# Another order for the first quarter of a hand-ordered linear-attention and MLP kernel

## The chip, the cores and the metric

The kernel runs on one core of a Trainium2 chip. A core has TensorE (PE), which multiplies matrices into PSUM, VectorE (DVE), ScalarE (ACT), GpSimd (POOL), which can't read PSUM here and works in SBUF, and SyncE (SP), which in this kernel only issues DMAs. Each engine takes its own instructions in the order in which they were emitted and waits at semaphores for the others. The time is device microseconds of one execution, as the median of several; smaller is better.

## The reference

```python
# attention with a complex decay, per batch b (4) and head h (8); S = 768 steps, D = 48
mag = sqrt(a_re**2 + a_im**2);  scale = min(mag, 0.999) / (mag + 1e-6)
a_re_n, a_im_n = a_re * scale, a_im * scale
for t in range(S):
    S_re, S_im = ar * S_re - ai * S_im + k_t (x) v_t,  ar * S_im + ai * S_re
    y[t] = q_t @ S_re
# then, on x = y laid out as (4, 768, 384), d_model = 384
xn = (x - mean) / sqrt(var + 1e-6) * g_ln
out = x + relu(xn @ w_ch1) @ w_ch2          # 384 -> 1536 -> 384
```

## The kernel before, in words

The step-by-step recurrence is done in chunks of 128 steps. Two chunks make a pair; there are twelve pairs, three for each batch. For a pair the kernel needs the running sum of log|a| and the running phase over the chunk. In the names of the order table, P is the pair, n the chunk:

- `are.P`, `aim.P`, `q.P.c`, `k.P.c`, `vf.P.c`: loads on SP's queue (L452 and L404). Pair 0 has `are`, `aim` and all that follows up to `ks` and `qs` in two halves of four heads, 0.0 and 0.1.
- On ScalarE `ln` (log of a_re, L459) and `iv` (its inverse, L461); `r` = a_im / a_re (L295); `r2` its square; `u` = log(1 + r2) on ScalarE (L473); `l` and `lc` on VectorE (L477, L480): log|a|, clamped.
- `dec` (L488): matmuls with a triangle of ones sum it up; `e` and `en` (L492) are exp of plus and minus the sum, on ScalarE.
- `th` = arctan(r) (L496); `ph` (L503, L507): matmuls sum the phase, in turns, on top of what the pair before carried over; `car` (L517, L520) carries it on; `sin` (L525), `qt` (L532, a quarter turn by a matmul) and `cos` (L536).
- `ke`, `qe` = k * en, q * e and `ks`, `qs` = these times cos and sin (all through the helper line L295). `kT`, `qT` transpose them on TensorE (L613), `ksT`, `qsT` copy the result from PSUM (L292 on VectorE, L290 on ScalarE).
- `am` (L636) are the scores of a chunk, `atm` (L295) the masked scores, `gm` (L660) and `G` the state, `gs` its sum ahead of the decay, `y` (L697, L700) the chunk's output. `row` (L592, a small DMA), `dps` (L597) and `decc` bring the pair's decay into place.
- `bn` (L707, L708) mean and variance, `x` (L714, L717), `xtr`, `xT` its transpose (L734), `mm1` (L767), `relu` (L779, L781), `mm2` (L791), `rstd`, `oa`, `xr`, `ot` and the store `st`.
- `wl.0` and `wl.1` (L369, L371): GpSimd issues the loads of the two weights, w1b and w2b, with a cast. `wc` (L385) multiplies w1b by the layer norm's gain on VectorE, in nine pieces; `mm1` needs them.
- `warm.*` (L822, L826): matmuls whose result nobody reads, in places of TensorE's order where it would wait. `tab.log` and `tab.trig` (L831): loads of ScalarE's function table; logarithms and exponentials are in one, arc tangents and sines in the other.

The order of everything is a table, the string PLAN. A token is `name:engine`, with the PSUM bank behind the engine's letter (P, A, V, G, S) and, behind an @, an operation for which this one must wait besides its own data. The program emits the operations in the table's order, each on the named engine, so the table is the order of every engine's queue. Names of some kinds that aren't in the table aren't emitted: where `qe.1.0.1` is missing, `qe.1.0.0` does both chunks.

Buffers are rings (`are` and `aim` three deep, `vf` two, `e` and `en` two, `ks` and `qs` three). TensorE's eight PSUM banks are given out by the table.

Of the kernel before, what the change touches and what calls it, by code (L numbers as in the profile page):

```python
# [49 lines left out]
r2.0.0:V warm.12:P6 th.0.1:A warm.w18:P5 r2.0.1:V uthc:V warm.w11:P4 pad.ks.0:G@r2.0.0 th.1.0:A warm.w9:P4 q.0.1:S  # L50
warm.8:P1 warm.7:P6 r2.1.0:G warm.w36:P2 warm.3:P4 warm.4:P6 ph.0.1:P0 aim.2.0:S warm.w6:P5 ph.0.0:P6 k.0.0:S v.0:G
tab.log.2:A u.0.1:A warm.w8:P2 warm.w13:P5 k.0.1:S u.0.0:A warm.2:P2 car0.1:G@uth l.0.1:V warm.w30:P3 warm.w38:P2
u.1.0:A mask:G@r2.0.0 l.0.0:V q.1.1:S zrow.0:G@uth pad.ks.1:G@r2.0.0 lc.0.1:V ln.2.0:A l.1.0:V dec.0.1:P1 warm.11:P2
warm.w17:P5 e.0.1:A1 k.1.1:S warm.w12:P3 lc.0.0:V iv.2.0:A lc.1.0:V dec.0.0:P7 qe.0.1.0:G@lc.0.0 car.0.0:V6 dec.1.0:P4
q.1.0:S car.0.1:V0 en.0.1:A1 r.2.0:V qrow:G warm.w16:P2 en.0.0:A7 ph.1.0:P2 e.1.0:A4 q.2.1:S ke.0.0.0:V e.0.0:A7
warm.28:P1 are.3.0:S r2.2.0:V en.1.0:A4 warm.19:P7 warm.w4:P1 ke.0.1.0:V vf.1.0:S u.2.0:A warm.w0:P5 qe.0.0.0:V
warm.w40:P4 warm.w22:P7 car.1.0:V2 warm.w3:P7 k.1.0:S warm.5:P7 warm.w20:P5 l.2.0:V warm.w31:P7 warm.w23:P5 aim.3.0:S
warm.w21:P7 warm.w28:P1 qe.1.0.0:V tab.trig.3:A sin.0.1:A0 sin.0.0:A6 lc.2.0:V qt.0.1:P0 ks.0.1.1:V sin.1.0:A2 row.0:S
qs.0.1.1:V warm.w2:P7 warm.w19:P4 ks.0.0.1:V row.1:S qt.0.0:P6 qe.1.0.1:V cos.0.1:A0 qt.1.0:P2 vf.1.1:S cos.0.0:A6
ks.0.1.0:V dec.2.0:P0 qs.0.1.0:V cos.1.0:A2 ks.0.0.0:V k.2.1:S warm.14:P6@en.1.0 qs.0.0.0:V qs.0.0.1:V warm.0:P6  # L60
kT.0:P4 th.2.0:A qs.1.0.0:V qT.0:P6 warm.w34:P7 wl.0:G@qs.0.0.1 kT.1:P3 ksT.0:V4 qT.2:P2 k.2.0:S qsT.0:V6 qT.1:P5
ke.1.0.0:G q.2.0:S tab.log.4:A en.2.0:A0 qsT.2:V2 am.0:P6 are.4.0:S ksT.1:V3 qsT.1:A5 atm.0:V6 warm.27:P3 ks.1.0.0:G
warm.w14:P3 e.2.0:A0 am.1:P2 atm.1:V2 ln.3.0:A y.0:P6 gm.0:P0 dps.1:P7 warm.15:P1 warm.w33:P1 G.0:A0 warm.16:P5
warm.25:P1 qT.3:P1 decc.1:A7 bn.0:V6 iv.3.0:A gm.1:P0 y.1:P5 qsT.3:V1 aim.4.0:S x.0:A6 dps.0:P4 r.3.0:G kT.2:P7
bn.1:V5 decc.0:A4 xtr.0:P4 kT.3:P6 ksT.2:V7 ph.2.0:P2 G.1:V0 qe.2.0.1:G@ksT.2 tab.trig.5:A th.3.0:A ksT.3:V6 am.2:P0
ngl:G@ksT.2 sin.2.0:A2 warm.w37:P7 v.1:G atm.2:V0 warm.13:P7 am.3:P6 xT.0:A4 qt.2.0:P2 r2.3.0:G@ksT.3 x.1:A5 gm.2:P4
atm.3:V6 ph.3.0:P0 cos.2.0:A2 xr.0:G G.2:V4 warm.23:P2 are.5.0:S xtr.1:P2 car.3.0:A0 warm.9:P3 warm.w41:P6 sin.3.0:A0
gm.3:P4 wc.0.1:V y.2:P7 wc.1.0:V y.3:P5 xT.1:A2 wc.1.1:V wc.1.2:V vf.2.0:S qt.3.0:P0 wl.1:G@wc.1.1 bn.2:V7
mm1.0.1.0:P2 cos.3.0:A0 wc.0.0:V mm1.0.1.1:P2 vf.2.1:S wc.0.2:V x.2:A7 wc.2.2:V mm1.0.0.1:P0 wc.2.0:V relu.0.1:A2
wc.2.1:V bn.3:V5 mm1.0.0.0:P0 qe.2.0.0:G@wc.2.1 xtr.2:P3 aim.5.0:S x.3:V5 mm1.0.2.0:P6 ke.2.0.0:G@bn.3 xT.2:V3  # L70
xtr.3:P5 mm1.0.2.1:P6 xT.3:V5 tab.log.6:A u.3.0:A gs.3:V4 mm1.1.0.1:P2 qs.2.0.0:V relu.0.2:A6 mm1.1.1.0:P4 ks.2.0.0:V
relu.0.0:A0 mm1.1.1.1:P4 ks.2.0.1:V mm1.1.0.0:P2 l.3.0:V ln.4.0:A mm1.1.2.1:P0 relu.1.1:A4 relu.1.0:V2 kT.5:P6
mm1.1.2.0:P0 iv.4.0:A ksT.5:V6 qT.5:P4 relu.1.2:A0 lc.3.0:V qT.4:P3 r.4.0:G@ksT.5 qsT.5:V4 kT.4:P5 qsT.4:A3 dec.3.0:P6
ksT.4:V5 are.6.0:S am.5:P0 e.3.0:A6 rstd.0:G am.4:P2 atm.5:V0 r2.4.0:A mm2.0.0:P4 mm2.0.1:P4 atm.4:V2 u.4.0:A q.3.0:S
rstd.1:G@atm.5 mm2.2.0:P1 ln.5.0:A row.3:S mm2.0.2:P4 l.4.0:V q.3.1:S v.2:A mm2.2.1:P1 G.3:G ot.0:V4 mm2.2.2:P1
iv.5.0:A lc.4.0:V k.3.1:S gm.4:P5 en.3.0:A6 dec.4.0:P2 r.5.0:G G.4:V5 y.4:P4 oa.2:A1 st.0:S y.5:P0 bn.4:V4 mm2.3.0:P7
ln.6.0:A k.3.0:S ot.2:G bn.5:V0 mm2.1.0:P6 en.4.0:A2 x.4:V4 mm2.3.1:P7 e.4.0:A2 st.2:S r2.5.0:V vf.3.1:S mm2.1.1:P6
qe.3.0.0:V x.5:A0 row.4:S xtr.4:P2 qe.3.0.1:V iv.6.0:A mm2.3.2:P7 vf.3.0:S xr.3:G@qe.3.0.0 xT.4:V2 xtr.5:P5 u.5.0:A
mm2.1.2:P6 xr.1:G@qe.3.0.1 q.4.0:S xT.5:V5 ke.3.0.1:G ot.3:V7 mm1.2.0.0:P4 ot.1:V6 mm1.2.0.1:P4 aim.6.0:S rstd.2:G
qs.3.0.0:V k.4.0:S mm1.2.2.0:P2 tab.trig.7:A th.4.0:A ke.3.0.0:V mm1.2.2.1:P2 k.4.1:S relu.2.0:A4 ks.3.0.0:V ph.4.0:P6  # L80
st.1:S relu.2.2:A2 st.3:S l.5.0:V qT.6:P0 q.4.1:S abs.4.0:A6 dps.4:P1 kT.6:P5 v.3:G@ks.3.0.0 qsT.6:V0 mm1.2.1.0:P2
are.7.0:S th.5.0:A decc.4:V1 ksT.6:V5 kT.7:P0 sin.4.0:A6 vf.4.0:S dps.3:P4 mm1.2.1.1:P2 decc.3:V4 car.4.0:A6 ksT.7:V0
qT.7:P5 relu.2.1:A2 lc.5.0:V am.6:P6 r.6.0:G@ksT.7 qsT.7:V5 gm.6:P4 ph.5.0:P0 cos.4.0:A atm.6:V6 vf.4.1:S G.6:A4
am.7:P2 sin.5.0:A0 gm.7:P4 q.5.0:S ke.4.0.0:G@atm.6 atm.7:V2 y.6:P5 mm2.4.0:P7 abs.5.0:A0 ke.4.0.1:G mm2.5.0:P6
th.6.0:A G.7:V4 q.5.1:S y.7:P2 bn.6:V5 cos.5.0:A qe.4.0.0:G@G.7 mm2.5.1:P6 are.8.0:S bn.7:V2 x.6:A5 mm2.5.2:P6
aim.7.0:S x.7:V2 mm2.4.1:P7 ks.4.0.0:V k.5.1:S xtr.7:P2 xtr.6:P5 mm2.4.2:P7 tab.log.8:A ln.7.0:A xT.7:V2 ksT.8:S
dec.5.0:P0 xT.6:V5 r2.6.0:A qs.4.0.0:V kT.9:P4 e.5.0:A0 mm1.3.1.0:P2 v.4:G@xT.6 aim.8.0:S ksT.9:V4 en.5.0:A0 qT.8:P5
xr.5:V qe.5.0.0:G qT.9:P4 k.5.0:S qsT.8:V5 u.6.0:A mm1.3.1.1:P2 qsT.9:V4 rstd.3:G mm1.3.2.0:P0 relu.3.1:A2 l.6.0:V
am.9:P4 k.7.1:S mm1.3.2.1:P0 qe.5.0.1:G iv.7.0:A atm.9:V4 mm1.3.0.1:P2 relu.3.2:A0 xr.4:G@qsT.9 mm1.3.0.0:P2 lc.6.0:V
# [773 lines left out]
```

## Time and profile before

| | us |
|---|---|
| median of three runs | 185.67 (185.29 to 185.86) |
| the profiled execution | 185.77 |
| its span in the trace | 184.1 |
| PE busy in the span | 174.6 (95%) |
| DVE busy | 154.6 (84%) |
| ACT busy | 154.9 (84%) |
| POOL busy | 111.4 (61%) |

The span runs from the first instruction to the last, and the 1.7 us between it and the execution's time lie around it. A busy share is a mean over stages: TensorE's contains the warm matmuls of the start, and what ends a stage is read from the waits and the order of time there. In rows of the order of time the columns are start, duration, engine, line, operation, output and inputs, shape, count (several instructions may be merged into one row), and in brackets the idle time ahead of it and what ended it.

### The profile page before, as it was taken

The numbers are of one execution on the slowest core, as the hardware profiler recorded it, in microseconds if no ns is written. First come the engines' busy times: TensorE is split into PE (matmuls) and PEld (weight loads), VectorE is DVE, ScalarE is ACT, GpSimd is POOL, SyncE is SP. The second block draws the span as 40 slices with busy tenths as digits, with TensorE's granted clock in tenths as the row PEclk, the third lists the DMA queues.
The fourth block names the chain that finished last, engine by engine and source line by source line (L and its number), as shares of the span: only waits on it lengthen the run. The fifth ranks groups of instructions, "written<-read, shape, count | busy, mean of one in ns | idle before, by whom it ended". The sixth has DMA issues, their size and how long they took to land.

```text
span 184.1 us, 5013 instructions
## 1 busy us (share of the span) xinstructions
PE 174.6 (95%) x1971; PEld 137.8 (75%) x1971; DVE 154.6 (84%) x274; ACT 154.9 (84%) x217; POOL 111.4 (61%) x124
## 2 busy tenths in 40 slices
...
GB/s 156 306 195 240 231 194 198 197 246 207 241 178 149 263 244 228 210 204 198 184 239 155 253 203 217 221 171 196 151 199 177 200 152 190 230 184 89 109 0 85
DMA packets 128791, 35.39 MB, mean 192 GB/s; under 512 B 124800, under 2 KB 128000, under 8 KB 128768
## 3 DMA queue, kind: packets, MB, share of 16 engines
...
q8 instruction: 15, 0.25, 0.5%
...
## 4 chain that ended last, share of the span: by engine, by line
PE 74%; DVE 9%; SPq 6%; POOL 4%; issue 3%; DMA 2%; DVEq 0%; POOLq 0%
PE banks L767 24%; PE banks L791 24%; PE banks L613 6%; PE banks L636 5%; SPq L452 3%; PE banks L488 3%; PE banks L507 3%; PE banks L697 2%; DMA k<-in_k_dram 2%; SPq L404 2%; PE banks L660 2%; PE banks L700 2%; PE banks L734 2%; POOL ke L295 2%; PE banks L503 1%
## 5 line engine op out<-in xcount | busy, mean ns | idle before, releaser
L791 PE MATMUL banks<-w2b,h 128*128 128x384 bf16 (+2 forms) x300 | 53.0, 319 | 0.1
L767 PE MATMUL banks<-xT,w1b 128*128 128x256 bf16 x432 | 51.5, 273 | 0.0
L767 PEld LDWEIGHTS <-w1b 128*128 128x128 bf16 x432 | 46.1, 114 | 1.2 <-DVE stats L707 0.3
L779 ACT ACTIVATE h<-banks 128x1024 bf16<-128x1024 f32 x31 | 31.5, 1022 | 11.7 <-PE banks L767 11.3
L791 PEld LDWEIGHTS <-h 128*128 128x128 bf16 x300 | 26.9, 97 | 13.9 <-issue 0.2
L295 DVE TENSOR_TENSOR atm<-banks,mask 128x1024 bf16<-128x1024 f32 x24 | 28.9, 1220 | 3.5 <-PE banks L636 3.0
L295 POOL TENSOR_TENSOR r<-aim,are 128x768 f16<-128x768 f32 x9 | 16.5, 1832 | 8.6 <-DVE ksT L292 7.5
L831 ACT ACT_TABLE_LOAD x15 | 19.2, 1283 | 1.0 <-PEq L847 0.8
L295 POOL TENSOR_TENSOR qe<-q,e 128x384 bf16<-128x384 f32 (+1 forms) x14 | 16.2, 1156 | 4.7 <-ACT e L492 1.7
L826 PE MATMUL banks<-u_e 128*128 128x512 f16 x42 | 14.1, 424 | 2.4 <-POOL u_e L323 2.2
L724 POOL TENSOR_SCALAR xr<-x,mv 128x384 f32<-128x384 bf16 x13 | 8.5, 658 | 11.0 <-ACT x L714 4.5
L707 DVE BATCH_NORM_STATS2 stats<-banks 128x6 f32<-128x384 f32 x24 | 13.4, 556 | 1.4 <-PE banks L700 1.2
L636 PE MATMUL banks<-qsT,ksT 128*128 128x128 bf16 x192 | 14.3, 219 | 0.0
L807 DVE SCALAR_TENSOR_TENSOR ot<-banks,rstd,xr 128x384 f32<-128x384 f32 (+2 forms) x18 | 10.4, 587 | 3.9 <-PE banks L791 3.3
L477 DVE SCALAR_TENSOR_TENSOR l<-r,w 128x768 f16<-128x768 f16 (+1 forms) x13 | 11.7, 908 | 2.3 <-ACT r L473 2.3
L636 PEld LDWEIGHTS <-ksT 128*128 128x128 bf16 x192 | 12.2, 98 | 1.6 <-DVE ksT L292 0.2
L414 POOL TENSOR_SCALAR v<-vf 128x768 bf16<-128x768 f32 x9 | 9.5, 1061 | 5.6 <-DVE mv L708 2.7
L805 POOL TENSOR_TENSOR ot<-ot,x 128x384 f32<-128x384 f32 x7 | 7.1, 1007 | 9.1 <-DVE atm L295 7.9
L697 PE MATMUL banks<-v,atm 128*128 128x48 bf16 x192 | 12.0, 183 | 0.2 <-DVE atm L295 0.2
L295 POOL TENSOR_TENSOR ke<-k,en 128x768 bf16<-128x768 f32 (+1 forms) x9 | 11.9, 1324 | 0.2
L459 ACT ACTIVATE w<-are 128x768 f32<-128x768 f32 (+1 forms) x13 | 10.2, 791 | 2.1 <-DMA are<-in_a_re_dram 2.1
L697 PEld LDWEIGHTS <-atm 128*128 128x128 bf16 x192 | 10.7, 96 | 1.4 <-DVE atm L295 0.6
...
## 6 DMA issues: line engine op xcount, KB each, us to landing
...
```

The source lines that it names most:

```text
L295: {"DVE": nc.vector, "POOL": nc.gpsimd}[eng(name)].tensor_tensor(**kw)
L477: nc.vector.scalar_tensor_tensor(out=S_("l"), in0=S_("r2"), scalar=0.5, in1=S_("w"), op0=ALU.mult, op1=ALU.add)
L613: nc.tensor.transpose(ps[:, h], T(nm, P)[:, c, h], ident)
L636: nc.tensor.matmul(ps[:, h], lhsT=T("ksT", n)[:, h], rhs=T("qsT", n)[:, h], start=True, stop=True)
L697: nc.tensor.matmul(ps[:, h], lhsT=T("atm", n)[:, h], rhs=T("v", P)[:, c, h], start=True, stop=nfirst)
L707: nc.vector.bn_stats(out=T("stats", n), in_=bank(f"y.{n}")[:, 0:DM])
L767: nc.tensor.matmul(ps[:, jj], lhsT=w1b[:, dc, ts(gi, JG * C)].rearrange("k (p j) -> k j p", j=JG)[:, jj], rhs=T("xT", P)[:, dc].rearrange( ...
L779: act(out=dst, in_=src, func=AF.Relu)
L791: nc.tensor.matmul(bank(f"o.{N}")[:, ws], lhsT=T("h", P)[:, j, ts(c, C)], rhs=w2b[:, j, ws], start=(j == 0), stop=(j == NJ - 1))
L807: nc.vector.scalar_tensor_tensor(out=o, in0=bank(f"o.{N}")[:, ws], scalar=T("rstd", P)[:, ds(c, 1)], in1=xs, op0=ALU.mult, op1=ALU.add)
L826: g.add(f"warm.w{i}", lambda i=i: nc.tensor.matmul(bank(f"warm.w{i}"), lhsT=u_e[:, 0, 0], rhs=u_e.rearrange("p c j t -> p (c j t)"), start ...
L831: g.add(f"tab.{nm}.{i}", lambda tab=tab: nc.scalar.preload_act_table_set(tab))
```

## The change

The table's early part is another one. From `y.4` on TensorE, `ln.6.0` on ScalarE and the second third of the table on the other engines, the engines' orders are the same in both; some waits behind an @ differ there. Here are the orders of the early part, engine by engine, worked out from the two tables (warm left out, GpSimd with its @):

```
ScalarE before: tab.log.0 ln.0.0 iv.0.0 ln.1.0 ln.0.1 iv.1.0 iv.0.1 tab.trig.1 th.0.0 th.0.1 th.1.0 tab.log.2 u.0.1
 u.0.0 u.1.0 ln.2.0 e.0.1 iv.2.0 en.0.1 en.0.0 e.1.0 e.0.0 en.1.0 u.2.0 tab.trig.3 sin.0.1 sin.0.0 sin.1.0 cos.0.1
 cos.0.0 cos.1.0 th.2.0 tab.log.4 en.2.0 qsT.1 e.2.0 ln.3.0 G.0 decc.1 iv.3.0 x.0 decc.0 tab.trig.5 th.3.0 sin.2.0 xT.0
 x.1 cos.2.0 car.3.0 sin.3.0 xT.1 cos.3.0 x.2 relu.0.1 tab.log.6 u.3.0 relu.0.2 relu.0.0 ln.4.0 relu.1.1 iv.4.0 ...
ScalarE after:  tab.log.0 ln.0.0 iv.0.0 ln.0.1 iv.0.1 u.0.0 ln.1.0 u.0.1 iv.1.0 e.0.0 en.0.0 e.0.1 en.0.1 ln.2.0 u.1.0
 iv.2.0 tab.trig.1 th.0.1 th.0.0 th.1.0 car.0.1 sin.0.1 sin.0.0 car.0.0 cos.0.1 cos.0.0 tab.log.2 u.2.0 en.1.0 e.1.0 G.0
 tab.trig.3 sin.1.0 th.2.0 cos.1.0 tab.log.4 ln.3.0 e.2.0 en.2.0 iv.3.0 tab.trig.5 sin.2.0 x.0 th.3.0 cos.2.0 xT.0 r2.3.0
 sin.3.0 car.3.0 x.3 x.2 xT.3 cos.3.0 tab.log.6 ln.4.0 u.3.0 iv.4.0 relu.0.0 relu.1.1 ksT.5 relu.0.2 relu.1.0 ...

VectorE before: uth r.0.0 r.0.1 r.1.0 r2.0.0 r2.0.1 uthc l.0.1 l.0.0 lc.0.1 l.1.0 lc.0.0 lc.1.0 car.0.0 car.0.1 r.2.0
 ke.0.0.0 r2.2.0 ke.0.1.0 qe.0.0.0 car.1.0 l.2.0 qe.1.0.0 lc.2.0 ks.0.1.1 qs.0.1.1 ks.0.0.1 qe.1.0.1 ks.0.1.0 qs.0.1.0
 ks.0.0.0 qs.0.0.0 qs.0.0.1 qs.1.0.0 ksT.0 qsT.0 qsT.2 ksT.1 atm.0 atm.1 bn.0 qsT.3 bn.1 ksT.2 G.1 ksT.3 atm.2 atm.3 G.2
 wc.0.1 wc.1.0 wc.1.1 wc.1.2 bn.2 wc.0.0 wc.0.2 wc.2.2 wc.2.0 wc.2.1 bn.3 x.3 xT.2 xT.3 gs.3 qs.2.0.0 ks.2.0.0 ...
VectorE after:  uth r.0.0 r2.0.0 r.0.1 r2.0.1 l.0.0 lc.0.0 l.0.1 lc.0.1 r.1.0 r2.1.0 l.1.0 r.2.0 lc.1.0 ke.0.0.0 r2.2.0
 decc.0 ke.0.1.0 qe.0.1.0 qe.0.0.0 ks.0.1.1 qs.0.0.1 ks.0.0.1 qs.0.1.1 ks.0.1.0 ks.0.0.0 qs.0.1.0 car.1.0 ksT.0 ksT.1
 l.2.0 qsT.1 lc.2.0 qsT.0 atm.1 atm.0 G.1 bn.1 ks.1.0.0 qs.1.0.0 x.1 ksT.3 ksT.2 qsT.3 xT.1 bn.0 G.2 qsT.2 atm.3 atm.2
 gs.3 bn.3 bn.2 wc.0.1 wc.0.2 wc.0.0 wc.1.0 wc.1.2 wc.2.1 wc.1.1 wc.2.2 qsT.4 xT.2 wc.2.0 qsT.5 relu.0.1 ks.2.0.0 ...

GpSimd before:  ... pad.ks.0@r2.0.0 r2.1.0 v.0 car0.1@uth mask@r2.0.0 zrow.0@uth pad.ks.1@r2.0.0 qe.0.1.0@lc.0.0 qrow
 wl.0@qs.0.0.1 ke.1.0.0 ks.1.0.0 r.3.0 qe.2.0.1@ksT.2 ngl@ksT.2 v.1 r2.3.0@ksT.3 xr.0 wl.1@wc.1.1 qe.2.0.0@wc.2.1
 ke.2.0.0@bn.3 r.4.0@ksT.5 rstd.0 rstd.1@atm.5 G.3 r.5.0 ...
GpSimd after:   ... pad.ks.0 car0.1 pad.ks.2 pick ngl qs.0.0.0@qs.0.1.0 v.0@qs.0.1.0 ke.1.0.0@lc.2.0 qe.1.0.0 wl.0
 v.1@qs.1.0.0 qe.2.0.0@qs.1.0.0 r.3.0 qs.2.0.1 qs.2.0.0 wl.1 ke.2.0.0@wc.2.0 r2.4.0@r.4.0 one rstd.1 r.5.0@xr.0 ...

SP before:      are.0.0 are.1.0 are.0.1 aim.0.0 aim.0.1 aim.1.0 are.2.0 vf.0.0 vf.0.1 gln q.0.0 q.0.1 aim.2.0 k.0.0
 k.0.1 q.1.1 k.1.1 q.1.0 q.2.1 are.3.0 vf.1.0 k.1.0 aim.3.0 row.0 row.1 vf.1.1 k.2.1 k.2.0 q.2.0 are.4.0 aim.4.0 ...
SP after:       are.0.0 are.0.1 aim.0.0 aim.0.1 are.1.0 aim.1.0 are.2.0 aim.2.0 k.0.1 k.0.0 row.0 q.0.0 q.0.1 gln vf.0.1
 vf.0.0 q.1.1 q.1.0 q.2.0 k.1.0 k.1.1 vf.1.1 are.3.0 q.2.1 vf.1.0 aim.3.0 k.2.0 k.2.1 are.4.0 aim.4.0 row.1 are.5.0 ...
```

On TensorE the order ahead of `y.4` follows these; 71 warm matmuls become 56 (42 wide and 29 narrow before, 49 and 7 after). `qT.4` and `qT.5` stand ahead of the first `mm1` instead of within its block. The core of the diff, its first lines (the rest of its table lines say the same as the orders above) and its code:

```diff
 PLAN = """
-ue:G are.0.0:S are.1.0:S are.0.1:S uth:V aim.0.0:S warm.w27:P0 pad.ks.2:G warm.1:P0 aim.0.1:S pad.qs.2:G warm.w1:P7
-aim.1.0:S warm.w7:P0 tab.log.0:A ln.0.0:A pick:G@uth warm.w29:P5 are.2.0:S iv.0.0:A warm.w32:P0 car0.0:G warm.w10:P7
...
+ue:G are.0.0:S are.0.1:S zrow.1:G uth:V warm.w0:P0 zrow.0:G car0.0:G aim.0.0:S warm.w1:P0 pad.qs.1:G aim.0.1:S
+warm.w2:P0 ident:G are.1.0:S warm.w3:P0 tab.log.0:A ln.0.0:A pad.qs.2:G warm.w4:P0 aim.1.0:S pad.ks.1:G iv.0.0:A
...
+iv.1.0:A l.0.1:V warm.w17:P0 warm.w18:P0 k.0.0:S warm.w19:P0 lc.0.1:V e.0.0:A6 r.1.0:V dec.0.1:P4 en.0.0:A6
+warm.w20:P0 e.0.1:A4 warm.w21:P0 warm.w22:P0 r2.1.0:V en.0.1:A4 warm.w23:P0 row.0:S warm.w24:P0 ln.2.0:A warm.w25:P0
...
-    for i in range(29):
+    for i in range(7):
         g.add(f"warm.{i}", lambda i=i: nc.tensor.matmul(
...
-    for i in range(42):
+    for i in range(49):
         g.add(f"warm.w{i}", lambda i=i: nc.tensor.matmul(
```

186 lines of the change are left out of this document (91 added, 95 removed).

## The prediction

> **What bounds the kernel now.** I read the page's head first, then the engines by stretch of time, then the chain of waits, then the order of time of each engine up to the point where the two order tables become the same.
>
> ```profile
> span 184.1 us, 5013 instructions
> PE 174.6 (95%) x1971; PEld 137.8 (75%) x1971; DVE 154.6 (84%) x274; ACT 154.9 (84%) x217; POOL 111.4 (61%) x124
> ...
> PE 74%; DVE 9%; SPq 6%; POOL 4%; issue 3%; DMA 2%; DVEq 0%; POOLq 0%
> ...
> 10.00:20.00 10.00, 7.98 (x51) 4.62 (x51) 7.42 (x16) 9.95 (x15) 5.55 (x10) 1.00 1.05 210
> 20.00:30.00 10.00, 8.76 (x104) 5.89 (x103) 9.94 (x21) 9.41 (x17) 5.70 (x3) 1.00 1.04 213
> 30.00:40.00 10.00, 10.00 (x155) 8.11 (x153) 9.53 (x23) 9.08 (x16) 7.06 (x9) 1.00 0.95 216
> 40.00:45.00 5.00, 5.00 (x51) 4.98 (x49) 4.31 (x9) 4.97 (x6) 2.06 (x2) 1.00 1.11 214
> 45.00:50.00 5.00, 5.00 (x68) 4.55 (x67) 4.34 (x7) 4.94 (x7) 2.64 (x3) 1.00 1.00 225
> 50.00:60.00 10.00, 10.00 (x104) 6.83 (x102) 8.71 (x18) 9.95 (x14) 7.45 (x9) 1.00 0.78 174
> ```
>
> The columns of the stretches are length, then busy PE, PEld, DVE, ACT, POOL, granted clock, DMA share, GB/s. From 40 us on TensorE is never idle, so there the end is set by how much matmul work is left. Before 40 us the fill-in matmuls (warm) make it look busy, while ScalarE (9.95 of 10) and then VectorE (9.94 of 10) carry the time. So the question is: when does TensorE begin its unbroken run, and how much work is left then. These rows answer it for the kernel before (the first from the chain of waits, the others from the engines' order of time):
>
> ```profile
> 12.57 4.25 DMA k<-in_k_dram
> ...
> 16.93 0.56 DVE L295 TENSOR_TENSOR ke<-k,en 128x384 bf16<-128x384 f32 x1 [0.19 <-DMA k<-in_k_dram]
> ...
> 36.31 1.13 DVE L385 TENSOR_SCALAR w1b<-w1b,ngl 128x512 bf16<-128x512 bf16 x4
> ...
> 24.15 1.00 POOL L369 DMA_DIRECT2D w1b<-in_moe_w_ch_dram  x1 [7.81 <-DMA row<-e]
> ...
> w1b<-in_moe_w_ch_dram POOLq DMA_DIRECT2D x1, 1152.0 KB, 12.0
> w2b<-in_moe_w_ch_dram POOLq DMA_DIRECT2D x1, 1152.0 KB, 10.6
> ...
> 37.98 2.81 PE L767 MATMUL banks<-xT,w1b 128*128 128x256 bf16 x24
> ...
> 54.29 0.19 PE L697 MATMUL banks<-v,atm 128*128 128x48 bf16 x1
> ```
>
> VectorE waits for the first k until 16.9, then is busy nearly throughout and starts wc (the scaling of w1b) at 36.31. The load of w1b, issued at 24.15, needs 12.0 us and so lands at 36.15: one instruction's length ahead of wc. The first mm1 starts at 38.0, and y.4, the first matmul from which TensorE's two orders are the same, at 54.29.
>
> **The change, part by part.**
>
> *ScalarE up to the cosines of pair 0.* Four tables are loaded by then before, two after. Pair 0's loads also move ahead of pair 1's on SP's queue.
>
> ```profile
> 3.00:4.50 1.50, 1.50 (x5) 0.44 (x3) 0.25 (x1) 1.05 (x2) 1.16 (x5) 1.00 1.13 295
> 6.00:7.50 1.50, 1.50 (x13) 1.06 (x11) 0.59 (x1) 1.50 (x4) 0.70 (x5) 1.00 1.13 311
> ...
> 3.35 0.52 ACT L459 ACTIVATE w<-are 128x384 f32<-128x384 f32 x1 [1.28 <-DMA are<-in_a_re_dram]
> 5.23 1.26 ACT L459 ACTIVATE w<-are 128x768 f32<-128x768 f32 x2 [0.80 <-DMA are<-in_a_re_dram]
> ...
> 10.64 1.28 ACT L831 ACT_TABLE_LOAD   x1
> 11.93 1.67 ACT L473 ACTIVATE r<-r 128x384 f16<-128x384 f16 x3
> ...
> 15.48 0.86 ACT L492 ACTIVATE en<-banks 128x384 bf16<-128x384 f32 x2
> ...
> 21.62 1.60 ACT L536 ACTIVATE trig<-banks 128x384 bf16<-128x384 int16 x3
> ```
>
> At some 300 GB/s a piece of 192 KB takes 0.65 us and 384 KB 1.3 us. The first piece lands at 3.35; are.0.1, aim.0.0 and aim.0.1 follow it, and pair 1's are, now fifth, would land at 3.35 + 3 x 0.65 + 1.3 = 6.6, with the lateness seen for the second load (5.23, where 3.35 + 1.3 = 4.65) at about 7.1. ScalarE needs it for ln.1.0, which now stands ahead of u.0.1, and waits for it half a microsecond. A half-tensor instruction steps by 0.42 us and a whole one by 0.75 (the second row of ln is one of each, 1.26, less 0.52 for the half). So 7.1 + ln.1.0, u.0.1, iv.1.0 (1.95) + four exponentials of pair 0 (1.6) + ln.2.0, u.1.0, iv.2.0 (2.25) + table (1.3) + three arc tangents (1.65, as the three of the row of u) + two car (0.55) + two sines and two cosines (1.65, with the step of a half) = 18.05. Before, the cosines' group ends at 23.2, with pair 1's in it: pair 0 is some 4 us earlier.
>
> *What it costs pair 1.* Its exponentials, sines and cosines come behind a second switch of tables, but the number of table loads up to tab.log.6 is seven in both. ScalarE gives up qsT.1, x.1, xT.1, relu.0.1 and both decc and takes two car, r2.3.0, x.3 and xT.3. From 18.05 its instructions up to tab.log.6 are four tables (5.2), sixteen whole-tensor ones (12.0) and seven half-size ones (3.1): that load would start at 38.35.
>
> ```profile
> 40.56 1.28 ACT L831 ACT_TABLE_LOAD   x1
> ```
>
> Before it starts at 40.56, so ScalarE, with 2.2 us in hand, ends no chain there.
>
> *VectorE.* It takes ks.1.0.0 from GpSimd, qsT.1, x.1, xT.1, relu.0.1 and two decc from ScalarE, and gives qs.0.0.0, qe.1.0.0 and qs.2.0.0 to GpSimd.
>
> ```profile
> 19.52 0.96 DVE L477 SCALAR_TENSOR_TENSOR l<-r,w 128x768 f16<-128x768 f16 x1
> ...
> 25.35 1.28 DVE L292 COPY qsT<-banks 128x1024 bf16<-128x1024 bf16 x2
> ...
> 27.14 2.35 DVE L295 TENSOR_TENSOR atm<-banks,mask 128x1024 bf16<-128x1024 f32 x2
> 29.40 0.56 DVE L707 BATCH_NORM_STATS2 stats<-banks 128x6 f32<-128x384 f32 x1
> ...
> 42.56 0.95 DVE L295 TENSOR_TENSOR qs<-qe,trig 128x1536 bf16<-128x1536 bf16 x1
> ```
>
> After cos.0.0 (18.05) VectorE has ks.0.0.0 and qs.0.1.0 to do (to 18.85), then car.1.0 and the copies ksT.0 and ksT.1 (0.5 + 0.6 + 0.6): l.2.0 starts at about 20.5, ScalarE's u.2.0 being done by 18.05 + 1.3 + 0.85 = 20.2. From there to bn.2 the new order gives, in steps: l 0.9, lc 0.3, six copies of 0.6 (qsT.1, qsT.0, ksT.3, ksT.2, qsT.3, qsT.2: 3.6), four atm 4.6, ks.1 and qs.1 1.8, four bn 2.8 (stats and aggregate, 0.7), G.1, G.2 and gs.3 1.5 (as ke, 0.5), x.1 and xT.1 0.8. That is 16.3, so VectorE is free for wc at 36.75 if nothing holds it.
>
> *GpSimd, and the step that decides.* The load of w1b now stands behind qs.0.0.0, v.0, ke.1.0.0 (which must wait for lc.2.0) and qe.1.0.0.
>
> ```profile
> 25.22 1.64 POOL L295 TENSOR_TENSOR ke<-k,en 128x768 bf16<-128x768 f32 x1
> 26.94 3.10 POOL L295 TENSOR_TENSOR ks<-ke,trig 128x1536 bf16<-128x1536 bf16 x1
> ```
>
> qs.0.0.0 is a quarter of the second row, 0.8, and starts when VectorE has done qs.0.1.0 at 18.85; qT.1 follows it at 19.65 and is done before qsT.1 has its turn at 21.35, so it is hidden by l.2.0; if it came 1.2 us later it would hold lc.2.0. lc.2.0 ends at 20.5 + 0.9 + 0.6 (qsT.1) + 0.3 = 22.3. ke.1.0.0 costs 1.64 and qe.1.0.0, of the same shape, the same: GpSimd issues w1b at 25.55, where before it was 24.15. With 12.0 us it lands at 37.55, after VectorE is free (36.75): VectorE stands still for 0.8 us, and qsT.4, xT.2 and relu.0.1 queue behind wc. Three wc of 0.28 give mm1 at 38.45 (before 37.98). The bounds of the load are 10.6 (that of w2b) and 12.0 with an issue a microsecond late; I take 12.0, since SP's queue has aim.4, are.4 and are.5 to carry beside it as before:
>
> ```profile
> q1 hardware_dynamic: 5838, 1.41, 47.3%
> q0 software_dynamic: 400, 1.18, 46.2%
> ```
>
> (These are the queues' shares from 24 to 38 us: two full queues, half each.) The load of w2b comes at about 35.5 (before 37.48) in the same queue, so behind w1b: 37.55 + 10.6 = 48.15 at the latest. Its cover is the mm1 block; mm2 starts at about 49. Were the cover gone, each microsecond would be one of TensorE.
>
> *SP, and what moves further on.* row.0 stands now between k.0 and q.0 on SP's queue, and all loads behind it wait for e.0.1 (done at 10.2 by the sums above). It costs nothing as long as q.0 is there by 15.9, when VectorE asks for it; each issue takes SP 0.4 to 1.5 us, and q.0 follows at 11 to 12. decc.0 stands before ke.0.1.0 on VectorE and dps.0 before dec.1.0 on TensorE; both want row.0's landing by about 14, and if it came later both engines would stand still for the difference. r.4.0 and G.3 go to VectorE, r2.4.0 to GpSimd and rstd.0 to ScalarE: all of them run during the mm1 and mm2 blocks, which hide them as long as kT.5 and dec.4.0 (below) are in time.
>
> *TensorE.* Fifteen fill-in matmuls fewer cost and bring nothing by themselves, since they stand where TensorE waits.
>
> ```profile
> 45.71 0.45 PE banks L613 x8
> ...
> 57.86 0.17 PE banks L734 x3
> ```
>
> From the first mm1 to y.4 the kernel before has 54.29 - 37.98 = 16.3 us without a hole. Of that, qT.4 and qT.5 (0.45 each) and xtr.3 (0.17) now stand ahead of mm1, in time that is empty, and dps.1, a single small matmul, comes in (put at 0.1): 15.35. Within it the nearest call is kT.5. Its ks.2.0.0 stands on VectorE behind nine wc (2.45), qsT.4, qsT.5, xT.2 (1.5) and relu.0.1 and ends 6 us after w1b lands:
>
> ```profile
> 45.23 1.22 DVE L781 TENSOR_SCALAR h<-banks 128x1024 bf16<-128x1024 f32 x1
> ```
>
> TensorE asks for it 0.9 + 5.4 = 6.3 us after that, the 5.4 being the eight blocks of mm1 and an xtr ahead of it: 0.3 to spare. dec.4.0, through r2.4.0 on GpSimd and u.4.0, has about as little.
>
> *The sum.* y.4 starts at 38.45 + 15.35 = 53.8, against 54.29: -0.5. Handovers between engines are counted at next to nothing above; the one that the rows show (k landed at 16.82, ke started at 16.93) took 0.11, and for those on the way to w1b I add 0.2: -0.3. Behind y.4 the orders are the same, and by the same counting the other engines reach that point earlier too, so TensorE keeps it. The profiled execution took 185.77 (span 184.1), 0.1 above the median of 185.67. The sum gives 185.47 for the one and 185.37 for the other; I say 185.4.
>
> *A rule against it.* VectorE and GpSimd get in each other's way:
>
> ```profile
> 49.09 0.23 POOL L753 TENSOR_SCALAR rstd<-mv 128x2 f32<-128x2 f32 x1
> ...
> 60.24 0.99 POOL L753 TENSOR_SCALAR rstd<-mv 128x2 f32<-128x2 f32 x1
> ```
>
> The same two-column operation takes 0.23 or 0.99, which I put down to what VectorE does beside it. The new table drops the forced turns (@) of most GpSimd operations before 20 us, so qs.0.0.0 and the fills may be hit; each such hit ahead of w1b costs up to 0.76, and two of them put the issue at 27.1, the late rival below. The Trainium skill's "GPSIMD Engine Reference", section Key points, says that the two contend where VectorE has two SBUF inputs or a two-port mode; the row agrees that there is such a cost, but not where it falls.
>
> **The rivals.** *w1b is no limit* (for it: the two loads differ by 1.4 us, and what runs beside them is not the same; against: both are long). Then VectorE's 36.75 decides: mm1 at 37.65, y.4 at 53.0, -1.3: 184.4 with the profiled time as base. *w1b is issued late: slower.* GpSimd's queue has ke.1.0.0 behind lc.2.0, which hangs on k.1, on ScalarE's u.2.0 and on qs.0.0.0 at GpSimd's pace; every delay goes to mm1 one for one, where the other chains have 0.8 us of room. From an issue at 26.6 on (1.05 later than counted) the kernel is slower by over 0.56; at 27.1 it takes 186.8. For it: the row of ks with 3.10 us, and a count that has no contention in it; against: loads of pair 0 land earlier. *The gain is lost again in the mm1 block*: kT.5 or dec.4.0 lose 0.3 to 0.5 us, no change, 185.7.
>
> **How the numbers follow.** A change can be told from none here beyond about 0.3%, 0.56 us. Forecast 0.37, w1b no limit 0.25, w1b late 0.25, lost again 0.13. Of the forecast's own spread (184.8 to 185.9) a third is faster by over 0.56 (185.1 and less), and of the late case nearly all is slower by that. Faster: 0.25 + 0.12 = 0.37; slower: 0.25; same: the rest, 0.38. The range reaches to w1b at 10.6 us with VectorE free a little sooner (184.1, from -1.3 and 0.3 for that) and to the late issue (186.8).
>
> **What would show it.** In the trace after: cos of pair 0 done by about 18; w1b issued at 25.5 and wc at about 37.6, behind idle time of VectorE that a DMA ends; first mm1 at 38.5; y.4 15.3 us later. The prediction is wrong if GpSimd issues w1b a microsecond off, if the load takes another time than 12 us, or if TensorE has holes behind mm1.

## The result, and the profile after

| kernel | us, median | runs | ratio to before (95%) |
|---|---|---|---|
| before | 185.69 | 7, 185.29 to 185.86 | |
| after | 186.55 | 7, 186.40 to 190.02 | 1.007 (1.0051 to 1.009) |

The changed kernel is 0.7% slower, 0.9 us, where 0.3 us less was forecast, and its runs lie further apart. Medians are of all runs; the ratios leave out runs more than 1.5% above the fastest of their kernel, and with them part of the scatter treated below, and one run of 204.67 at a granted clock of 0.854 is left out of the ranges too.

The profile after, from its page: span, busy times, the shares of the chain of waits, and then the stretches of the early part (length, busy PE, PEld, DVE, ACT, POOL, granted clock, DMA share, GB/s).

```profile
span 184.6 us, 4985 instructions
PE 176.0 (95%) x1956; PEld 136.3 (74%) x1956; DVE 158.3 (86%) x279; ACT 153.9 (83%) x215; POOL 99.6 (54%) x119
...
PE 67%; ACT 12%; DVE 6%; POOL 5%; issue 4%; DMA 3%; SPq 1%; POOLq 0%; DVEq 0%; ACTq 0%
```
```profile
10.00:20.00 10.00, 8.84 (x55) 4.82 (x55) 8.28 (x20) 9.88 (x18) 0.25 (x1) 1.00 0.98 197
20.00:30.00 10.00, 9.26 (x131) 6.44 (x129) 9.81 (x16) 9.91 (x13) 6.27 (x6) 1.00 1.07 222
30.00:40.00 10.00, 9.30 (x131) 6.75 (x128) 9.81 (x24) 9.63 (x15) 7.84 (x6) 1.00 1.09 237
```

ScalarE has come into the chain: 12%, where it had no share before. It is busy for 29.4 of the first 30 us from 10 on, and the DMA share stays at about 1 all that time. The steps of the prediction can be read off in the order of time, engine by engine:

```profile
7.99 0.84 ACT L457 ACTIVATE w<-are 128x768 f32<-128x768 f32 x1 [1.22 <-DMA are<-in_a_re_dram]
...
18.34 0.88 ACT L534 ACTIVATE trig<-banks 128x384 bf16<-128x384 int16 x2
...
21.93 0.95 DVE L475 SCALAR_TENSOR_TENSOR l<-r,w 128x768 f16<-128x768 f16 x1
...
23.39 0.35 DVE L478 TENSOR_SCALAR l<-l 128x768 f16<-128x768 f16 x1
...
24.25 1.64 POOL L293 TENSOR_TENSOR ke<-k,en 128x768 bf16<-128x768 f32 x1 [2.51 <-DMA k<-in_k_dram]
27.44 0.99 POOL L367 DMA_DIRECT2D w1b<-in_moe_w_ch_dram  x1
33.80 3.32 POOL L293 TENSOR_TENSOR qs<-qe,trig 128x768 bf16<-128x768 bf16 x2
...
38.01 2.19 DVE L383 TENSOR_SCALAR w1b<-w1b,ngl 128x512 bf16<-128x512 bf16 x8
...
37.18 1.07 PE L611 MATMUL banks<-ident,qs 128*128 128x128 bf16 x16
38.94 0.84 PE L765 MATMUL banks<-xT,w1b 128*128 128x256 bf16 x6
54.44 0.19 PE L695 MATMUL banks<-v,atm 128*128 128x48 bf16 x1
```

and from the page's list of DMA issues (KB, us to landing):

```profile
w1b<-in_moe_w_ch_dram POOLq DMA_DIRECT2D x1, 1152.0 KB, 10.5
```

The first mm1 starts at 38.94 (37.98 before) and y.4 at 54.44 (54.29). Three chains reach mm1 almost together: VectorE is free for wc at 37.92, w1b lands at 27.44 + 10.5 = 37.94, and qs.2 on GpSimd ends at 37.12, behind which TensorE does qT.4, qT.5 (to 38.25), qt.3 and xtr.3. The early part thus gives +0.15 us in this pair of profiles. The rest is lost later: the last `ot` on VectorE starts at 181.45 instead of 180.64 (before, then after):

```profile
180.64 0.35 DVE L807 SCALAR_TENSOR_TENSOR ot<-banks,rstd,xr 128x128 f32<-128x128 f32 x1 [0.26 <-PE banks L791]
```
```profile
181.45 0.35 DVE L805 SCALAR_TENSOR_TENSOR ot<-banks,rstd,xr 128x128 f32<-128x128 f32 x1 [0.25 <-PE banks L789]
```

From y.4 to there it takes 180.64 - 54.29 = 126.35 us before and 181.45 - 54.44 = 127.01 after. These two numbers, y.4 and the **later stretch**, split each run below. (Behind the last `ot` the profile before has 0.3 us more left than the one after, so the spans, 184.1 and 184.6, differ by 0.5 and not by the 0.81 between these rows.)

Behind y.4 the tables differ in three things that I had passed over. (1) 47 **turns**: a turn is an operation's wait behind an @, and all 47 are on GpSimd. (2) On SP the store st.2 stands ahead of st.0 and of the load k.3.0. (3) The small table u_thc (uec on GpSimd, uthc on VectorE) is made at 57 and 75 us, where the kernel before made it in the head.

### The profile page after: what moved, and what is told of

The parts are those of the page before. It is cut to its first block, busy times and chain, and to the rows that moved or that the text cites. A ratio compares the mean times of both kernels' runs of the same rounds, so it can differ in the third digit from the quotient of the medians.

```text
span 184.6 us, 4985 instructions
## 1 busy us (share of the span) xinstructions
PE 176.0 (95%) x1956; PEld 136.3 (74%) x1956; DVE 158.3 (86%) x279; ACT 153.9 (83%) x215; POOL 99.6 (54%) x119
## 4 chain that ended last, share of the span: by engine, by line
PE 67%; ACT 12%; DVE 6%; POOL 5%; issue 4%; DMA 3%; SPq 1%; POOLq 0%; DVEq 0%; ACTq 0%
PE banks L765 24%; PE banks L789 21%; PE banks L611 5%; PE banks L634 4%; ACT L829 3%; DMA are<-in_a_re_dram 3%; PE banks L505 2%; PE banks L486 2%; PE banks L695 2%; POOL qs L293 2%; ACT th L494 2%; PE banks L698 2%; PE banks L732 2%; PE banks L658 1%; POOL r L293 1%
## 5 line engine op out<-in xcount | busy, mean ns | idle before, releaser
L777 ACT ACTIVATE h<-banks 128x1024 bf16<-128x1024 f32 x30 | 30.4, 1021 | 11.7 <-PE banks L765 11.7
L293 POOL TENSOR_TENSOR qe<-q,e 128x384 bf16<-128x384 f32 (+1 forms) x13 | 15.6, 1197 | 4.1 <-ACT h L777 1.6
L293 POOL TENSOR_TENSOR r<-aim,are 128x768 f16<-128x768 f32 x8 | 14.5, 1816 | 5.7 <-DVE xr L722 3.8
L824 PE MATMUL banks<-u_e 128*128 128x512 f16 x49 | 14.9, 449 | 2.2 <-POOL u_e L321 2.2
L412 POOL TENSOR_SCALAR v<-vf 128x768 bf16<-128x768 f32 x9 | 7.7, 851 | 9.3 <-DVE qe L293 4.2
L471 ACT ACTIVATE r<-r 128x768 f16<-128x768 f16 (+1 forms) x13 | 10.3, 793 | 2.0 <-POOL r L293 1.2
L722 POOL TENSOR_SCALAR xr<-x,mv 128x384 f32<-128x384 bf16 x12 | 7.1, 595 | 9.0 <-DVE stats L705 5.3
```

Source lines behind the costliest of these rows:

```text
L293: {"DVE": nc.vector, "POOL": nc.gpsimd}[eng(name)].tensor_tensor(**kw)
L777: act(out=dst, in_=src, func=AF.Relu)
L824: g.add(f"warm.w{i}", lambda i=i: nc.tensor.matmul(bank(f"warm.w{i}"), lhsT=u_e[:, 0, 0], rhs=u_e.rearrange("p c j t -> p (c j t)"), start ...
```

## The experiments

All were run with five rounds beside the kernel before, whose median was 185.55 to 185.79 each time. "Later part" tells which of the three things are as before (old) or as changed (new). y.4 and the stretch are those of the one profiled execution, which may lie off the median (both_8_turns_old: 185.32 in the profile, 186.97 in the median).

| run | early part | turns, SP, u_thc | median us | ratio (95%) | y.4 | stretch |
|---|---|---|---|---|---|---|
| before | old | old, old, old | 185.69 | | 54.29 | 126.35 |
| after | new | new, new, new | 186.55 | 1.007 (1.0051 to 1.009) | 54.44 | 127.01 |
| late_turns_old | new | old, new, new | 188.37 | 1.0149 (1.0122 to 1.0176) | 54.61 | 128.22 |
| v4_turn_old | new | v.4 old, new, new | 188.25 | 1.0119 (1.0085 to 1.0154) | 54.21 | 127.37 |
| before_uthc_late | old | v.4 new, old, new | 186.16 | 1.0031 (1.0017 to 1.0044) | 53.92 | 126.99 |
| v4_old_wl_early | new, wl.0 first | v.4 old, new, new | 193.52 | 1.0351 (1.0308 to 1.0393) | 59.53 | 129.07 |
| uthc_early | new | v.4 old, new, old | 187.24 | 1.0075 (1.0046 to 1.0105) | 55.41 | 127.08 |
| st0_first | new | new, old, new | 186.48 | 1.0046 (1.0026 to 1.0066) | 54.38 | 127.01 |
| both_early | new | v.4 old, old, old | 186.92 | 1.0068 (1.0037 to 1.0099) | 55.08 | 126.69 |
| tail_as_before | new | old, old, old | 185.55 | 0.9976 (0.9954 to 0.9997) | 54.10 | 126.16 |
| turns_and_st0 | new | old, old, new | 188.11 | 1.01 (1.006 to 1.014) | 55.00 | 128.24 |
| turns_and_uthc | new | old, new, old | 187.33 | 1.0031 (0.9993 to 1.007) | 54.13 | 127.97 |
| before_new_turns | old | 44 new, old, old | 186.67 | 1.0053 (1.0029 to 1.0076) | 53.91 | 127.34 |
| before_8_turns | old | 8 new, old, old | 186.64 | 1.006 (1.0035 to 1.0084) | 54.03 | 127.24 |
| both_8_turns_old | new | 8 old, old, old | 186.97 | 1.005 (1.002 to 1.008) | 54.03 | 126.26 |
| tail_old_k1_first | new, k.1 first | old, old, old | 185.46 | 0.9983 (0.9953 to 1.0013) | 54.39 | 126.20 |
| tail_old_wl_between | new, wl.0 earlier | old, old, old | 186.82 | 1.0046 (1.0014 to 1.0078) | 54.73 | 126.17 |
| tail_old_u_first | new, u.0.1 first | old, old, old | 186.81 | 1.0039 (1.0007 to 1.007) | 55.46 | 127.50 |
| tail_old_xT22_te | new | old, old, old; xT.22 | 185.62 | 0.9993 (0.997 to 1.0015) | 54.59 | 126.31 |
| after_xT22_te | new | new, new, new; xT.22 | 187.03 | 1.0069 (1.0047 to 1.0092) | 54.58 | 127.48 |

### The first four: one suspect at a time

*late_turns_old*, the 47 turns set back:
```
- xr.4:G@l.6.0   r.7.0:G@lc.6.0   v.4:G@uthc  ...
+ xr.4:G@qsT.9   r.7.0:G          v.4:G@xT.6  ...   (47 in all)
```


> The changed table, but the 47 forced turns (@) of GpSimd operations behind y.4 that differ are set back to those of before; the early part stays changed. Theory (a forced turn behind y.4, not the early part, costs most of the loss): the hole of TensorE near 80 us is gone and the time comes to 0.1 to 0.2 us above before, about 185.85 (0.7 below the changed kernel). Rival (the early part's lateness is carried on and costs it all): no change, about 186.5.

*v4_turn_old*, only `v.4:G@uthc` back to `v.4:G@xT.6`:

> The changed table with one token edited: v.4 waits for xT.6 as before, instead of for uthc. Theory (this single turn costs 0.8): 185.85, like the kernel with all late turns set back; in the trace v.4 of pair 4 starts at about 74 instead of 75.2 and VectorE's ot of chunk 5 no longer waits for xr. Rival (the turns cost it together): 186.2 to 186.4. Second rival (the early part): 186.5.

*before_uthc_late*, the kernel before with uec moved to before st.2, uthc to before ksT.9, and `v.4:G@uthc`:

> The kernel before, with two constants moved to the places that they have in the changed table (uec on GpSimd behind ot.2, uthc on VectorE ahead of ksT.9) and v.4 made to wait for uthc. Theory: 0.7 to 0.9 slower than before, about 186.45, with the early part untouched. Rival (the turn is harmless by itself): within 0.2 of before.

*v4_old_wl_early*, v4_turn_old with wl.0 ahead of ke.1.0.0 on GpSimd:

> As v4_turn_old, and the load of w1b is issued ahead of ke.1.0.0 and qe.1.0.0, at about 21.7 instead of 27.4. The prediction's step (w1b's landing decides when mm1 starts): w1b lands by 33 to 34 and mm1 starts earlier, y.4 up to 0.5 earlier. Theory from the trace (VectorE frees at 37.9 and GpSimd's qs.2 with qT.4, qT.5 reach mm1 at the same 38.9): not faster than v4_turn_old by more than 0.1; it may be slower, since ke.1.0.0 and qe.1.0.0 come a microsecond later behind the issue only if k is there by then.

Both theories about the turns fell: setting turns back alone made it worse, 188.4 and 188.3. The late u_thc costs about half a microsecond in the kernel before. And the early w1b costs 5.3 us against v4_turn_old in the medians. Between the two profiles it is 5.32 us ahead of y.4 and 1.70 behind it, nearly all of the latter a late transfer that is treated below. GpSimd's, SP's and TensorE's order of time there:

```profile
33.87 0.82 POOL L412 TENSOR_SCALAR v<-vf 128x768 bf16<-128x768 f32 x1 [6.78 <-issue]
...
24.63 6.32 SPq L450 DMA_DIRECT2D aim<-in_a_im_dram  x1
...
34.75 0.48 PE L658 MATMUL banks<-v,ks 128*128 128x48 bf16 x8 [3.48 <-POOL v L412]
...
44.06 0.82 PE L765 MATMUL banks<-xT,w1b 128*128 128x256 bf16 x6
```

v.1, which runs at 29.14 in tail_as_before below, starts at 33.87, after 6.78 us for which the row names no releaser. The lists of DMA issues show what it waited for: the load of vf.1.0, issued at 23.54 here and at 23.71 in v4_turn_old, takes 10.2 us to land instead of 3.7, so it lands at 33.7 (these two lists, and then the stretch from 35 to 40 us in both):

```profile
vf<-in_v_dram SPq DMA_DIRECT2D x1, 192.0 KB, 10.2
...
vf<-in_v_dram SPq DMA_DIRECT2D x1, 192.0 KB, 3.7
...
35.00:40.00 5.00, 5.00 (x56) 3.86 (x54) 2.98 (x4) 1.80 (x3) 4.94 (x4) 0.50 1.06 265
...
35.00:40.00 5.00, 4.85 (x69) 3.64 (x65) 4.75 (x15) 4.81 (x10) 2.52 (x3) 1.00 1.13 282
```

I read this as w1b's bytes taking the place of other loads'. TensorE stands 3.48 us for v.1, and behind that its granted clock is 0.50 from 35 to 40 us (1.00 in v4_turn_old). v.1 is 4.6 us later than in v4_turn_old and mm1 5.35; that the clock made the difference is likely, and not shown. The issue of aim.3 holds SP for 6.3 us (1.08 in tail_as_before), but a long issue alone is no sign of the damage: every profile has one of 4.2 to 6.6 us behind w1b's, the kernel before one of 6.20 at 26.42.

### Undoing the three things singly and together

*uthc_early*, *st0_first*, *both_early*, *tail_as_before*, from the changed kernel:
```
+ pick:G uec:G ... r2.1.0:V uthc:V ... v.4:G@xT.6                    (uthc_early, both_early)
- uec:G st.2:S r2.5.0:V ... st.0:S qe.3.0.0:V k.3.0:S
+ uec:G r2.5.0:V ... st.0:S qe.3.0.0:V k.3.0:S st.2:S                (st0_first, both_early)
                                both, and the 47 turns set back      (tail_as_before)
```

> The changed kernel with one thing undone: the small table uthc is made early again (uec on GpSimd right behind pick, uthc on VectorE right behind r2.1.0, where the changed kernel's VectorE waits 1.48 us from 11.6), and v.4 takes its turn from xT.6 as before. Theory A (the late uthc, 0.14 to 0.85 us on VectorE at 74.9 in its busiest stage, is what costs TensorE 0.8 us between 73 and 90): about 185.85, TensorE level with the changed kernel's +0.15 all the way. Theory B (the loads that SP issues 1.5 to 4 us late from 57 on cost it): no gain, 186.5 or the 188 of the kernel in which only v.4's turn was set back.

> The changed kernel with one thing undone: on SP the store st.0 and the load k.3.0 stand ahead of the store st.2 again, which waits for GpSimd's ot.2 at 56.2. Theory B: st.0 goes out at 55 to 56, k.3.0 and what follows up to 2 us earlier, the late holes between 80 and 88 go, about 185.9, and the runs lie closer together than the changed kernel's 186.4 to 190.0. Theory A: unchanged, 186.5.

> Both of these undone together. Theory A alone or B alone: the same time as the one of the two that helps, about 185.85. If each holds a part: less than either alone. If neither holds: 186.5 or more, and what is left are the turns and the state in which the head hands over.

> Both undone, and the 47 turns that differ behind y.4 set back to the kernel before's as well: the changed kernel's early part with the later part of the kernel before. If nothing but the later part costs the 0.8 us (theories A, B and the turns together), this gives the kernel before plus what y.4 shows in the changed kernel, +0.15: 185.85, and near it in every run. If the early part hands over more than y.4 shows (what GpSimd, ScalarE or SP still has to do at 54 us), it stays at 186.5 or above, as the kernel with the turns alone set back did (188.37).

*turns_and_st0* and *turns_and_uthc* are tail_as_before with u_thc, or with SP's order, left as changed. *before_new_turns* is the opposite test, in the kernel before, with 44 of the 47 turns (three name an operation that stands behind theirs in the old order).

> The changed kernel with the 47 later turns and SP's order (st.0 and k.3.0 ahead of st.2) set back to the kernel before's, uthc left late. Measured by the stretch from y.4 to the last ot on VectorE: 126.35 us in the kernel before, 127.01 in the changed one, 128.22 with the turns alone set back, 126.16 with turns, SP order and uthc set back. If SP's order is what the turns need: 126.2 here, about 185.6. If uthc is: 128, about 187.8. If both: between.

> The counterpart: the 47 turns and the early uthc set back, SP's order left as changed. If SP's order is what the turns need: 128 us behind y.4, about 187.8. If uthc is: 126.2, about 185.6.

> The kernel before with 44 of the changed kernel's 47 later turns (three name an operation that stands behind theirs in the old order), nothing else: its own early part, SP order and uthc. If the changed turns cost time by themselves: 127 us or more behind y.4 (126.35 before), 186.4. If they are as good as the old ones and only fail together with the late loads: 126.35, 185.8.

With all three back the stretch is 126.16, as before or a little less, and the median is level with the kernel before (185.55 against 185.79 beside it), though its twelve runs go from 184.47 to 188.38. Any one of them left new costs in it, by one profile each: u_thc 2.1 us with the old turns (turns_and_st0), SP's order 1.8 of which 1.4 are another thing (below), the turns 0.5 (both_early) and 1.0 (before_new_turns). They don't add up, since after, with all three new, loses 0.7: the new turns fit the late u_thc, and the old ones don't. With the old turn v.4 runs beside u_thc, which then takes 0.85 us (turns_and_st0); with the new one v.4 waits for it, and it takes 0.22 (after). Neither theory A nor B alone was right.

SP's order shows in two rows. VectorE's order of time and SP's, in turns_and_uthc, then in tail_as_before:

```profile
57.14 0.84 SPq L811 DMA_DIRECT2D out_dram<-ot  x2
59.81 1.14 DVE L805 SCALAR_TENSOR_TENSOR ot<-banks,rstd,xr 128x384 f32<-128x384 f32 x2 [0.73 <-DMA out_dram<-ot]
```
```profile
55.01 0.36 SPq L811 DMA_DIRECT2D out_dram<-ot  x1
58.96 1.15 DVE L805 SCALAR_TENSOR_TENSOR ot<-banks,rstd,xr 128x384 f32<-128x384 f32 x2
```

The first row has both stores: st.2 at 57.14, which waits for GpSimd, and st.0 behind it at 57.60, 2.6 us later than in tail_as_before. An `ot` that takes the buffer of a stored one waits 0.73 for that store, and TensorE, matmul by matmul, is 0.4 behind from 66 us on. In after this wait is 0.38 and costs TensorE nothing: st0_first, without it, has the same 127.01.

### Which turns

*before_8_turns* gives the kernel before eight of the new turns, *both_8_turns_old* takes them out of both_early, where v.4 has its old turn already, so seven:
```
  v.4:G@xT.6      qe.5.0.0:G      rstd.3:G      qe.5.0.1:G        (old)
  v.4:G@uthc      qe.5.0.0:G@xr.5 rstd.3:G@xr.5 qe.5.0.1:G@l.6.0  (new)
  xr.4:G@qsT.9    r.7.0:G         r2.7.0:G@G.8      r.8.0:G@abs.6.0   (old)
  xr.4:G@l.6.0    r.7.0:G@lc.6.0  r2.7.0:G@qs.5.0.0 r.8.0:G           (new)
```

> The kernel before with eight changed turns on GpSimd and nothing else: v.4@uthc (uthc is done early here, so no wait of its own), qe.5.0.0@xr.5, rstd.3@xr.5, qe.5.0.1@l.6.0, xr.4@l.6.0, r.7.0@lc.6.0, r2.7.0@qs.5.0.0, r.8.0 without one. Theory: these carry the loss of the 44: GpSimd reaches xr.4 about 0.8 us later, VectorE's ot.4 waits 0.5 for it, 127.3 us from y.4 to the last ot, 186.6. Rival (the loss is spread over the turns behind 92 us): 126.35, 185.6.

> The changed kernel with uthc early and st.0 ahead of st.2, and only these eight turns set back, 39 left changed. Theory: as with all 47 set back, 126.2 us behind y.4, about 185.5. Rival: as with none set back, 126.7, 186.9.

Eight of the 44 carry all that the 44 lost: 127.24 against 127.34, 186.64 against 186.67. Taking them out of both_early gives 126.26 in its profile, as the theory said, but the median stays at 186.97, as the rival said. The profiled execution was the fastest of the twelve; how much of the others is the scatter treated next is not shown. So the eight are shown to carry the loss in the kernel before, and only by one profile behind the new early part. The same place in the kernel before (POOL, then VectorE), in before_8_turns, and in after with the hole on TensorE:

```profile
78.93 0.58 POOL L724 TENSOR_SCALAR xr<-x,mv 128x384 f32<-128x384 bf16 x1
79.34 0.39 DVE L480 TENSOR_SCALAR l<-l 128x768 f16<-128x768 f16 x1
79.65 1.12 DVE L807 SCALAR_TENSOR_TENSOR ot<-banks,rstd,xr 128x384 f32<-128x384 f32 x2
```
```profile
79.72 0.68 POOL L724 TENSOR_SCALAR xr<-x,mv 128x384 f32<-128x384 bf16 x1
79.18 0.77 DVE L480 TENSOR_SCALAR l<-l 128x768 f16<-128x768 f16 x1
80.43 1.14 DVE L807 SCALAR_TENSOR_TENSOR ot<-banks,rstd,xr 128x384 f32<-128x384 f32 x2 [0.49 <-POOL xr L724]
```
```profile
80.07 0.68 POOL L722 TENSOR_SCALAR xr<-x,mv 128x384 f32<-128x384 bf16 x1
79.50 0.81 DVE L478 TENSOR_SCALAR l<-l 128x768 f16<-128x768 f16 x1
80.78 1.14 DVE L805 SCALAR_TENSOR_TENSOR ot<-banks,rstd,xr 128x384 f32<-128x384 f32 x2 [0.48 <-POOL xr L722]
81.45 0.36 PE L658 MATMUL banks<-v,ks 128*128 128x48 bf16 x8 [0.29 <-DVE ot L805]
```

With the new turns GpSimd reaches xr.4 0.8 to 1.1 us later, now beside VectorE's lc.6.0, which takes 0.8 instead of 0.4; ot.4 waits 0.5 for xr.4, and gm.8 on TensorE waits 0.29 for the bank that ot frees. The loss is made in this place: matched by its matmuls from y.4 on, TensorE is level with before at 72.7 us, 0.24 behind at 80, and 0.75 to 0.98 behind at 88 to 94; from 100 us on it is 0.84, and 0.66 at the last `ot`.

### The early part and the scatter

*tail_old_k1_first* moves the load q.2.0 behind k.1.1 on SP, *tail_old_wl_between* moves wl.0 ahead of qe.1.0.0 on GpSimd, *tail_old_u_first* moves u.0.1 ahead of ln.1.0 on ScalarE, each in tail_as_before:

> The version with the changed early part and the old later part (185.55), and on SP the loads k.1.0 and k.1.1 ahead of q.2.0. In seven profiles of this early part the first mm1 came 11.3 to 11.9 us behind wl.0's issue, and that waits for ke.1.0.0, which waits for k.1 (2.1 to 3.1 us). Theory C (k.1's landing sets wl.0, so the first mm1 and the scatter): wl.0 at 26.3 instead of 27.3, the first mm1 up to 0.5 earlier (then the qs.2 chain on GpSimd and bn.2 end last), 185.1. Rival (the transfers share a full set of DMA engines, so an earlier w1b only delays others): no gain, or a loss as with wl.0 moved ahead of ke.1.0.0.

> The version with the old later part (185.55), with wl.0 on GpSimd ahead of qe.1.0.0 but behind ke.1.0.0: its issue 1.6 us earlier, at 25.7, which is where the prediction had it. If w1b's issue sets the first mm1, as in nine profiles of this early part (11.3 to 11.9 us behind it): 38.2 instead of 38.6 to 39.9, held then by bn.2 on VectorE and qs.2 on GpSimd, 185.2 and less scatter. Rival (the DMA engines are full from 10 to 45 us, so w1b's bytes delay those of k.2, vf.1 and aim.3): first mm1 later, up to the 6 us that wl.0 ahead of ke.1.0.0 lost.

> The same version with u.0.1 ahead of ln.1.0 on ScalarE, where ln.1.0 waits 1.2 us for are.1.0: u.0.1 fills the wait, and ScalarE's chain to cos.0.0 ends about 0.5 earlier (18.7 instead of 19.2). If ScalarE's chain still sets the end of the early part, y.4 comes 0.3 to 0.5 earlier, 185.1; if the loads and wl.0 do, no change, 185.5.

None made the early part faster: their y.4 of 54.39, 54.73 and 55.46 lie within, or just above, the 54.03 to 55.41 of the twelve profiles without these edits. With k.1 earlier, ke.1.0.0 started at 24.02 all the same (24.10 in tail_as_before), now behind VectorE's lc.2.0, and wl.0 left at 27.21. With wl.0 at 25.61, where the prediction had it, mm1 still came at 39.25:

```profile
25.61 0.99 POOL L367 DMA_DIRECT2D w1b<-in_moe_w_ch_dram  x1
...
26.64 1.65 POOL L293 TENSOR_TENSOR qe<-q,e 128x768 bf16<-128x768 f32 x1
...
27.20 1.92 DVE L293 TENSOR_TENSOR ks<-ke,trig 128x1536 bf16<-128x1536 bf16 x1
...
38.29 2.16 DVE L383 TENSOR_SCALAR w1b<-w1b,ngl 128x512 bf16<-128x512 bf16 x8
39.25 0.82 PE L765 MATMUL banks<-xT,w1b 128*128 128x256 bf16 x6
```

wc has no wait for the load there: it took 11.6 us, to 37.2, and VectorE came later. The reason is in the rows: qe.1.0.0 on GpSimd, now behind the issue, runs beside VectorE's ks.1.0.0, which takes 1.92 us instead of 0.94 (tail_as_before). Without that VectorE would have been free at 37.4 and mm1 have started at about 38.4 (an estimate from these rows; 38.60 in tail_as_before). So this run doesn't refute theory C (wl.0 sets mm1): the edit gained the load and lost as much beside it. In tail_old_u_first, ln.1.0 started at 8.35 without idle time and the cosines of pair 0 ended at 19.48, not earlier than in those twelve (18.65 to 19.59).

*tail_old_xT22_te* and *after_xT22_te* replace the DMA transpose of chunk 22, which the last mm1 group needs:
```
- xT.22:S
+ xtr.22:P3 xT.22:A3
```
The reason was a row of tail_old_u_first, here with the same group in tail_as_before:

```profile
174.80 4.12 PE L765 MATMUL banks<-xT,w1b 128*128 128x256 bf16 x36 [1.14 <-DMA xT<-x]
```
```profile
172.13 4.09 PE L765 MATMUL banks<-xT,w1b 128*128 128x256 bf16 x36
```

> The version with the changed early part and the old later part, and xT.22 no longer transposed by a DMA: three more matmuls (xtr.22, 0.33 us from the rows of the other xtr) on TensorE and a copy on ScalarE, which is idle there. Theory: the last wait goes, which half of the runs have, for 0.2 to 0.3 us of TensorE in every run: lowest about 184.8, median 185.6, nothing over 187. Rival (the scatter is all in the early part): the same spread of 3 to 4 us as without, all runs 0.2 to 0.3 higher.

> The changed kernel with only this edit. Theory: its runs, 186.4 to 190.0 so far, come to 186.5 to 187.3, median 186.7. Rival: the spread stays, median 187.

The runs lie at 184.91 to 187.06 (11) instead of 184.47 to 188.38 (12), and at 186.76 to 187.90 (6) instead of 186.40 to 190.02 (7). That the edit narrowed them is likely, but 6 and 11 runs don't show it. The wait itself is shown: it is in three of the eighteen profiles in which a DMA transposes chunk 22, with 1.14 us (tail_old_u_first), 1.22 (turns_and_uthc) and 1.38 (v4_old_wl_early), and their stretches of 127.50, 127.97 and 129.07 contain it. The medians are no better (185.62 and 187.03). Why the transfer is late in some runs wasn't found: its issue takes the same 1.19 us in both cases.

The other part is y.4, which lies at 54.03 to 55.41 in the twelve profiles with the new early part (unedited but for the place of u_thc), at 53.91 to 54.29 in the four with the old one. In all twelve it follows the first wc by 16.43 to 16.45 us, and in eight of them the row of wc shows 0.18 to 0.78 us of idle time that the load of w1b ends. Here tail_as_before and, with the latest y.4, uthc_early:

```profile
37.66 2.19 DVE L383 TENSOR_SCALAR w1b<-w1b,ngl 128x512 bf16<-128x512 bf16 x8 [0.23 <-DMA w1b<-in_moe_w_ch_dram]
...
38.97 1.14 DVE L383 TENSOR_SCALAR w1b<-w1b,ngl 128x512 bf16<-128x512 bf16 x4 [0.78 <-DMA w1b<-in_moe_w_ch_dram]
```

So in these eight w1b's landing sets y.4; in the other four w1b lands and VectorE comes free within 0.4 us of each other.

## Why the prediction was wrong

- *Failed: "Behind y.4 the orders are the same, and by the same counting the other engines reach that point earlier too, so TensorE keeps it."* I took the same order on each engine for the same time. The turns, st.2 on SP and u_thc had been left out of the sum; with them the stretch goes from 126.35 to 127.01, +0.66 of the +0.81 between the two profiles. tail_as_before shows it: the new early part with the old later part takes 126.16 and, in the median, 185.55. The stretch repeats from program to program: 126.16 to 126.20 in tail_as_before, tail_old_k1_first and tail_old_wl_between, 127.01 in after and again in st0_first.
- *Failed: the start of ScalarE's chain.* ln.1.0 started at 7.99, since are.1.0 landed then and not at 7.1 (1.22 us of idle time); pair 0's cosines ended at 19.22 instead of 18.05, and VectorE was busy almost without a break behind them: l.2.0 started 1.4 us late (21.93 instead of 20.5), lc.2.0 ended 1.4 late (23.74 instead of 22.3), and VectorE was free for wc at 37.92 instead of 36.75. In twelve profiles y.4 has a mean of 54.55, in the four of the old early part 54.04, where I had 54.0 (53.8 and 0.2 for the handovers) against 54.29: the early part is half a microsecond slower, not 0.3 faster. Its gain on paper hung on loads that move with the order: pair 0's loads went ahead, and pair 1's came later.
- *Two misses that cancelled: w1b.* GpSimd issued it at 27.44 instead of 25.55. Of these 1.9 us, 1.4 are the late lc.2.0, so ScalarE's start again; the other 0.5 are k.1, a DMA which I had moved on SP and not followed up to its user, for which ke.1.0.0 still waited at 23.74. (In tail_old_k1_first, with k.1 earlier, lc.2.0 alone gave 27.21.) The load took 10.5 us instead of 12.0. It landed at 37.94 against 37.55. The late rival had "at 27.1 186.8", close to the measured time by luck, for its way didn't happen: an issue 1.5 us late with a 12 us load. (With the forecast's own 0.2 for the handovers it should have said 186.9.)
- *Right in most profiles: the step that decides.* In after itself w1b lands as VectorE comes free, where the prediction had VectorE stand still for 0.8 us. In eight of the twelve profiles wc does wait for w1b.
- *Right: the mm1 block.* From the first mm1 to y.4 it took 15.5 us (15.35 predicted, 16.3 before), in all twelve profiles between 15.47 and 15.51. kT.5 and dec.4.0 made no hole.
- *The page's rule, too narrow where I used it.* I had weighed VectorE against GpSimd only ahead of w1b; the place where it cost was 80 us. lc.6.0 took 0.38 us in tail_as_before, 0.81 in after and 1.40 in turns_and_st0, where it ran beside r.7.0 on GpSimd (80.38 to 82.20) and where xr.4 took 1.28 instead of 0.58 beside VectorE's l.6.0 (78.51 to 79.96). The Trainium skill's "GPSIMD Engine Reference", section 1. Specifications, says that GpSimd shares its SBUF interfaces with VectorE and that they contend where VectorE has two SBUF inputs or a two-port mode. The rows agree that both are slowed (lc.6.0 has one input, and no row shows its mode), and only the runs told where it falls. The "Trainium Architecture — The Big Picture" of the Trainium skill, section What this means for kernel authors, calls it an exclusive lock and not a split bandwidth. The rows of turns_and_st0 fit that: lc.6.0 ends at 82.42, 0.22 us behind r.7.0, as if it had waited for it to end; no run was made to test it.
